# Two pairs of feature blocks of the sixth tile by seven half-size products, laced with the fifth tile's outputs

## The chip, the cores and the metric

The kernel runs on one core of a Trainium2 chip. The metric is the time of one execution on the device in microseconds (us); the median of several runs is compared. Engines are called by the names that the profile uses: PE is TensorE (matrix products), DVE is VectorE, ACT is ScalarE, POOL is GpSimd, SP is SyncE, which issues nearly all DMA transfers here.

## The reference

```python
def _attn_ref(q, k, v):                      # 4 batches, 8 heads, 768 steps, 64 channels
    gamma = 1.0 - 2.0 ** (-5.0 - np.arange(H))
    for t in range(S):
        state = gamma * state + einsum('bhd,bhe->bhde', k[:, :, t], v[:, :, t])
        y[:, :, t] = scale * einsum('bhd,bhde->bhe', q[:, :, t], state)

def _moe_ref(x, w_a, w_b, w_out):            # 3072 tokens, 512 wide, 1536 features
    a = x @ w_a
    b = x @ w_b
    return a * b @ w_out

x = attn_out.transpose(0, 2, 1, 3).reshape(B * S, H * D)
```

A decaying linear attention makes x, and x goes through a bilinear feed-forward layer: two products of x with a weight each, multiplied element by element, and a third product back to 512 columns.

## The kernel before

**Tiles.** The 3072 tokens are 24 slots of 128. Slots are gathered into tiles (`TILES = [4, 2, 2, 2, 2, 4, 8]`), so the sixth tile, index 5, has 4 slots (512 tokens, slots 12 to 15), and the seventh, `BIG`, has 8. For each slot q and k are scaled on GpSimd (`casts`, line 293), transposed by a DMA on SP (`flip`, line 312), and the loads of slot t+2 are issued behind that flip on SP. `turn(new, old)` (line 404) makes the masked scores of two slots (on PE, then four multiplications with the mask on VectorE, line 348), updates the state, and finishes two older slots, whose result is copied by ScalarE into `xt`, the input of the feed-forward layer.

**Feed-forward blocks.** The 1536 features are 12 blocks of 128. `ffn_a` (line 529) makes a block of a: four products on PE, which ScalarE casts into `asb`. `ffn_g` (line 543) makes the block of b in the same way, and VectorE multiplies it with `asb` into `ht`. `blocks(J, a, b)` runs both over blocks a to b.

**Seven products in place of eight.** For the outputs of the tiles of index 1 to 6, and for the whole of the first two products of `BIG`, the kernel uses the Strassen-Winograd scheme: the operands are cut in two each way, and the four quarter results come from seven products of sums of quarters, not from eight. `Group` (line 632) does it for the output of two slots: p1 to p7 are the products, A, B and C its three PSUM banks, `snap` copies a partial sum out of bank A on ScalarE, and VectorE adds a snap to a bank. `hsum` makes its sums of quarters of `ht`, `weight_sum` those of the third weight. `Unit` (line 786) does it for a pair of feature blocks of `BIG` (p and p+6) and one weight, 512 tokens wide; its weight sums `WS` are made on GpSimd by `weight_piece` (line 751), from a list of 32 pieces that `weight_pieces(n)` works off, and its input sums by `x_sum` on VectorE.

**Order.** All work is put in program order by hand: each engine runs its instructions in the order in which the code emits them (`seq`, line 100). PE's banks are eight: three in a ring (`psff`, line 75, which hands out the bank that has been free the longest), four of attention (y0, y1, at0, at1) and one for the state. `single(4, ...)` (line 736) runs the one output group of the fifth tile with blocks 0, 1 and 2 of the sixth between its products; then come blocks 3 to 11 of the sixth tile between the last turns, and `big()` with its two written orders START and END.

The main sequence around the change, before:

```python
    casts(19)
    single(4, Y0, AT0, FF)
    v_cast(18)
    casts(20)
    casts(21)
    blocks(5, 3, 5)
    v_cast(19)
    blocks(5, 5, 6)
    weight_pieces(6)
    turn(18, 16)
    sums(5, 5)
    casts(22)
    blocks(5, 6, 9)
    casts(23)
    weight_pieces(2)
```

Of the kernel before, what the change touches and what calls it, by code (L numbers as in the profile page):

```python
# [22 lines left out]
       "S02 S01 b7 a2 b2 S04 a6 b6 S13 a5 b5 S12 a3 b3 a4 b4 S11 c7 d7 c6 d6 S14 c5 d5 "  # L23
       "c3 c4 d4 d3")
V_LATE = range(12, 20)
LOADS = "p0 p1 w0 w1 a1 b1 a2 k2 q2 b2 v2 o0 o1 o2 o3 o4 o5 s6 t8".split()


@with_exitstack
def kernel(  # L30
# [29 lines left out]
    const = ctx.enter_context(tc.tile_pool(name="const", bufs=1))  # L60
    wpool = ctx.enter_context(tc.tile_pool(name="wpool", bufs=1))
    wstage = ctx.enter_context(tc.tile_pool(name="wstage", bufs=6))
    raw = ctx.enter_context(tc.tile_pool(name="raw", bufs=3))
    nat = ctx.enter_context(tc.tile_pool(name="nat", bufs=6))
    tra = ctx.enter_context(tc.tile_pool(name="tra", bufs=4))
    xtp = ctx.enter_context(tc.tile_pool(name="xtp", bufs=2))
# [39 lines left out]
        return bi  # L106


    raws, wst, whole = {}, {}, {}

    def load_slot(t, names="kqv"):
        b, ci = divmod(t, NCH)
        for nm in names:
            src = {"k": k, "q": q, "v": v}[nm]
            if nm == "q":
                if t % 2 == 0:
                    load_two(nm, src, b, ci // 2, t)
                continue
            if t % 2 == 0:
                whole[nm] = raw.tile([P, 2, H, D], F32, tag=nm + "f", name=nm + "f")  # L120
# [6 lines left out]
            load_slot(u, names)  # L127

    def load_two(nm, src, b, u, t):
        f = raw.tile([P, H, 2, D], F32, tag=nm + "f", name=nm + "f")  # L130
# [273 lines left out]
    def turn(new, old, eng=nc.scalar):  # L404
        if old is not None:
            ys[old // 2] = [psat.tile([P, 2, 2, 2, P // 2], F32, tag=f"y{r}", name="y") for r in range(2)]
        two = new is not None and (new + 1) % NCH < NCH - 1
        if new is not None:
            if two or old is None:
                update(new, eng)  # L410
            scores(new + 1, "y" if old is None else "ff")
            scores(new, "at")
        if old is not None:
            inter(old)
            inter(old + 1)
# [152 lines left out]
    def ffn_out(J, i, n):  # L568
        if n == 0:
            store()  # L570
            plain_out[i] = psff.tile([P, DM], F32, tag="ff", name="o")
        o = plain_out[i]
        for ft in range(NP * n, NP * n + NP):
            seq(nc.tensor.matmul(o, ht[J][:, ft, i * P : (i + 1) * P], wo_bf[:, ft],  # L574
                                 start=(ft == 0), stop=(ft == NFT - 1), skip_group_check=True))
# [10 lines left out]
    def tt(dst, x, y, op, eng=nc.vector):  # L586
        seq(eng.tensor_tensor(dst, x, y, op=op))  # L587
# [13 lines left out]
    hs = {}  # L601

    def hs_tile(J, s):
        if (J, s) not in hs:
            pool, tag = (raw, ("kf", "qf", "vf", "kf")[s - 1]) if J in (0, (BIG, 1)) else (wstage, "w")
            bufs = {}
            if (J, s) == (0, 4):
                pool, tag, bufs = tra, "kqT", {"bufs": 3}
            hs[J, s] = pool.tile([P, NP, 2, P], BF16, tag=tag, name=f"hs{s}", **bufs)

    def hsum(J, s, a, b, eng=nc.vector):
        U = slice(int(J == 0), 2 if isinstance(J, tuple) else TILES[J] // 2)
# [8 lines left out]
    def hsums(J, a, b, eng):  # L621
        for s in (2, 1, 4):
            hsum(J, s, a, b, eng)

    WHEN = {5: ["302"], 6: ["324"], 7: ["346"], 8: ["102"], 9: ["202d", "224", "124"],
            10: ["402", "424"], 11: ["246", "146", "446"]}

    def sums(J, ft, eng=nc.vector):
        for what in WHEN.get(ft, []):
            hsum(J, *map(int, what[:3]), nc.vector if what[3:] else eng)  # L630
# [102 lines left out]
    Y0, Y1, AT0, AT1 = ((psat, x) for x in ("y0", "y1", "at0", "at1"))  # L733
    ST = (psst, "st")

    def single(J, A, B, C):
# [12 lines left out]
    WS, XS, pieces = {}, {}, []  # L749

    def weight_piece(w, n, a, b):
        if (w, n) not in WS:
            WS[w, n] = raw.tile([P, 2, NP * P], BF16, tag=("kf", "qf", "vf")[len(WS) % 3], name=f"ws{w}{n}")
# [3 lines left out]
        S = {x: WS[w, x][:, :, a * P : b * P] for x in (1, 2, 3, 4) if (w, x) in WS}  # L757
        x, y, op = {3: (A11, A21, ALU.subtract), 2: (A22, S[3], ALU.subtract), 1: (A21, A22, ALU.add),
                    4: (A12, S.get(2), ALU.subtract)}[n]
        tt(S[n], x, y, op, nc.gpsimd)  # L760
# [25 lines left out]
    class Unit:  # L786
# [6 lines left out]
        def product(self, bank, left, right, first):  # L793
            if first:
                pool, tag = self.tags[bank]
                self.bank[bank] = pool.tile([P, 4 * P], F32, tag=tag, name="u" + bank)
            m, p = self.bank[bank], self.p
            for k in range(2):
                if isinstance(left, int):
                    w = WS[self.w, left][:, k, p * P : (p + 1) * P]  # L800
# [53 lines left out]

        def p4(self):
            self.product("B", (1, 1), XS[4], False)
            self.leave(1, 0, "B", 1)

    STEP = {"1": 0, "6": 4, "2": 6, "5": 8, "7": 9, "3": 12, "4": 17}
# [99 lines left out]
    def blocks(J, a, b):  # L959
        for ft in range(a, b):  # L960
            ffn_ab(J, ft)
            if J == 5 and ft + 1 < b:
                sums(J, ft, G_ if ft > 8 else nc.vector)

    def three(J, ft):
        store()
# [5 lines left out]
    def v_cast(t):  # L972
        cast(nc.scalar, vb[t], raws["v", t])
# [123 lines left out]
```

## Time and profile before

| | before |
|---|---|
| median of 3 runs | 219.35 us (218.97 to 219.61) |
| the profiled execution's own time | 219.35 us |
| its span (first to last instruction) | 217.6 us |
| PE busy | 210.5 us, 97% of the span |
| VectorE, ScalarE, GpSimd busy | 141.4, 100.8, 148.1 us |
| granted TensorE clock | 9 tenths or more in all 40 slices |

The profile is one execution, recorded by the hardware. A row of the timeline gives the start and the length in us, the engine, the source line, the operation with output<-input, the shapes, the number of instructions merged into the row, and in brackets the idle time of the engine ahead of it with what ended it. Rows of groups give busy time and the mean duration in ns after the bar. A row of a stretch (from:to) gives its length, then busy time of PE, PEld (weight loads), DVE, ACT and POOL, then the granted clock, the DMA share and GB/s. Matmuls are pipelined: the duration of one is longer than the distance from one to the next.

### The profile page before, as it was taken

Reading aid. Unit: us, or ns where it says so; the run is one execution under the profiler, and the core shown is the slowest. Engines: PE = TensorE matmul, PEld = TensorE weight load, DVE = VectorE, ACT = ScalarE, POOL = GpSimd, SP = SyncE. Lnnn points to the kernel's source line nnn. Section 1 sums busy time; section 2 is a strip of 40 time slices with the busy share of each in tenths; the row PEclk is TensorE's granted clock in tenths of the full one; section 3 lists DMA queues with packets and bytes.
Section 4 is the critical chain, followed back from the end, with each engine's and each line's share of the span. In section 5 each row is a group of like instructions: output and inputs, shape, how many; then the busy total and the mean of one; then the engine's idle time right before and its main releaser. Section 6 shows DMA issues by size and latency. Waiting matters only on the chain.

```text
span 217.6 us, 5674 instructions
## 1 busy us (share of the span) xinstructions
PE 210.5 (97%) x2244; PEld 143.5 (66%) x2244; DVE 141.4 (65%) x258; ACT 100.8 (46%) x221; POOL 148.1 (68%) x173
## 2 busy tenths in 40 slices
PE   7699999999999999999999999999999999999994
PEld 3457445587458888888888665456864444458883
DVE  2777446845973486356477245886586887688962
ACT  3266335343224444455576344455546656652331
POOL 5266876879344469579865949999999999950000
PEclk9999999999999999999999999999999999999999
DMA  6999999999999999999999997980013000000055
GB/s 165 290 322 364 384 289 362 384 270 229 207 265 230 191 236 213 195 218 254 198 216 247 206 202 182 255 124 5 3 48 145 0 2 3 0 2 0 27 193 169
DMA packets 85162, 39.68 MB, mean 182 GB/s; under 512 B 57488, under 2 KB 78864, under 8 KB 85136
## 3 DMA queue, kind: packets, MB, share of 16 engines
q1 hardware_dynamic: 84992, 39.26, 80.1%
q8 instruction: 17, 0.28, 0.6%
q10 hardware_dynamic: 144, 0.07, 0.1%
q14 instruction: 9, 0.07, 0.1%
HBM read 28.31 MB, written 6.29 MB: 159 GB/s over the span
## 4 chain that ended last, share of the span: by engine, by line
PE 91%; SPq 4%; DMA 3%; POOL 0%; issue 0%; DVE 0%
PE a L537 20%; PE g L549 19%; PE mA L654 12%; PE uA L805 10%; PE mB L654 6%; PE o L574 5%; PE uB L805 5%; SPq L132 4%; DMA wsta<-in_moe_w_a_dram 3%; PE mC L654 3%; PE at L342 2%; PE uC L805 2%; PE y L390 2%; PE st L360 2%; PE y L380 1%; PE y L500 1%
## 5 line engine op out<-in xcount | busy, mean ns | idle before, releaser
L551 DVE TENSOR_TENSOR ht<-g,asb 128x256 bf16<-128x256 f32 (+1 forms) x74 | 37.2, 503 | 37.5 <-PE g L549 34.4
L537 PE MATMUL a<-xt,wa_bf 128*128 128x256 bf16 (+1 forms) x296 | 52.7, 305 | 0.1
L549 PE MATMUL g<-xt,wb_bf 128*128 128x256 bf16 (+1 forms) x296 | 52.5, 304 | 0.0
L540 ACT CAST asb<-a 128x256 bf16<-128x256 f32 (+1 forms) x74 | 32.3, 437 | 38.8 <-PE a L537 35.7
L549 PEld LDWEIGHTS <-wb_bf 128*128 128x128 bf16 x296 | 28.6, 98 | 12.5
L537 PEld LDWEIGHTS <-wa_bf 128*128 128x128 bf16 x296 | 28.0, 98 | 12.1 <-POOL wa_bf L245 0.4
L286 POOL TENSOR_TENSOR kqb<-kf,ktab 128x512 bf16<-128x512 f32 x22 | 23.0, 1049 | 16.3 <-DMA kf<-in_k_dram 15.9
L812 ACT COPY snap<-uA 128x512 f32<-128x512 f32 x36 | 20.0, 588 | 15.4 <-PE uA L805 13.9
L654 PEld LDWEIGHTS <-hs 128*128 128x128 bf16 x234 | 22.8, 98 | 4.1
L286 POOL TENSOR_TENSOR kqb<-qf,qtab 128x512 bf16<-128x512 f32 x18 | 19.0, 1054 | 6.1 <-DMA qf<-in_q_dram 6.1
L348 DVE TENSOR_TENSOR aT<-at,mask 128x512 bf16<-128x512 f32 x36 | 22.3, 682 | 0.3
L661 ACT COPY snaps<-mA 128x256 f32<-128x256 f32 x30 | 11.0, 374 | 20.1 <-PE mA L654 20.1
L654 PEld LDWEIGHTS <-ht 128*128 128x128 bf16 x180 | 17.5, 98 | 3.2
L587 POOL TENSOR_TENSOR hs<-ht,hs 128x384 bf16<-128x384 bf16 (+1 forms) x17 | 16.7, 990 | 2.9 <-DVE ht L551 2.8
L587 POOL TENSOR_TENSOR ht<-gsb,asb 128x512 bf16<-128x512 bf16 x13 | 15.3, 1185 | 1.6 <-DVE gsb L587 1.6
L587 POOL TENSOR_TENSOR hs<-ht 128x384 bf16<-128x384 bf16 (+2 forms) x12 | 13.8, 1153 | 3.4 <-DVE ht L551 3.4
L245 POOL CAST vb<-vf 128x512 bf16<-128x512 f32 x16 | 10.0, 642 | 7.7 <-DMA vf<-in_v_dram 7.5
L654 PE MATMUL mA<-wsum,hs 128*128 128x256 bf16 x120 | 15.2, 273 | 0.0
L587 DVE TENSOR_TENSOR osb<-mB,snaps 128x256 f32<-128x256 f32 x20 | 8.5, 423 | 8.4 <-PE mB L654 4.2
L574 PE MATMUL o<-wo_bf,ht 128*128 128x512 bf16 x48 | 10.7, 379 | 0.0
L587 DVE TENSOR_TENSOR asb<-uB,snap 128x512 bf16<-128x512 f32 x12 | 8.2, 686 | 3.4 <-ACT snap L812 1.7
L587 DVE TENSOR_TENSOR gsb<-uB,snap 128x512 bf16<-128x512 f32 x12 | 8.3, 688 | 2.8 <-ACT snap L812 2.0
(101 smaller groups left out, 334.1 us busy)
## 6 DMA issues: line engine op xcount, KB each, us to landing
qf<-in_q_dram SPq DMA_DIRECT2D x12, 512.0 KB, 6.1
out_dram<-osb SPq DMA_DIRECT2D x21, 256.0 KB, 4.1
kf<-in_k_dram SPq DMA_DIRECT2D x18, 256.0 KB, 4.9
vf<-in_v_dram SPq DMA_DIRECT2D x18, 256.0 KB, 5.4
wsta<-in_moe_w_a_dram SPq DMA_DIRECT2D x6, 512.0 KB, 7.6
wsto<-in_moe_w_out_dram SPq DMA_DIRECT2D x6, 512.0 KB, 8.7
wstb<-in_moe_w_b_dram SPq DMA_DIRECT2D x5, 512.0 KB, 8.2
kf<-in_k_dram SPq DMA_DIRECT2D x3, 512.0 KB, 7.6
```

The lines of the kernel that those rows point to most:

```text
L286: seq(eng.tensor_tensor(dst, src, tab, op=ALU.mult))
L348: seq(nc.vector.tensor_tensor(aT[t][:, r], at[r], mask.to_broadcast([P, HP, P]), op=ALU.mult))
L537: seq(nc.tensor.matmul(a, wa_bf[:, kt, fs], xcols(J, kt, c0, c1), start=(kt == 0), stop=(kt == KT - 1)))
L540: seq(nc.scalar.copy(asb, a))
L549: seq(nc.tensor.matmul(g, wb_bf[:, kt, fs], xcols(J, kt, c0, c1), start=(kt == 0), stop=(kt == KT - 1)))
L551: seq(nc.vector.tensor_tensor(ht[J][:, ft, c0:c1], g, asbs.pop((J, ft, c0)), op=ALU.mult))
L574: seq(nc.tensor.matmul(o, ht[J][:, ft, i * P : (i + 1) * P], wo_bf[:, ft], start=(ft == 0), stop=(ft == NFT - 1), skip_group_check=True))
L587: seq(eng.tensor_tensor(dst, x, y, op=op))
L654: seq(nc.tensor.matmul(m, w, right[:, j], start=(first and j == 0), stop=(j == NP - 1), skip_group_check=True))
L661: seq(nc.scalar.copy(self.snaps[:, n], self.bank["A"]))
L805: seq(nc.tensor.matmul(m, w, right[:, k], start=(first and k == 0), stop=(k == 1), skip_group_check=True))
L812: seq(nc.scalar.copy(self.snaps[n], self.bank["A"]))
```

## The change

Four feature blocks of the sixth tile, 0 and 6, 1 and 7, are taken out of `blocks` and made by a new class `Quad`: one pair of blocks, one weight, seven products of half size (256 tokens wide, two matmuls each). Quads a and b are the two weights of the first pair, c and d those of the second. They stand in one written order, LACED, with the seven products of the fifth tile's output group (m1 to m7) and blocks 2 and 3 of the sixth (F is `ffn_a`, G is `ffn_g`). X is a sum of input quarters on VectorE, S is `casts`, V is `v_cast`, H is `hsum`. Blocks 4, 5 and 8 follow after the turn, blocks 9 to 11 as before.

A quad has a bank A of the ring, a bank B (AT1 or Y1), and shares one ring bank C between the a and b of a pair. Its snaps are copies on ScalarE, its adds are on VectorE; each b quad multiplies its halves with the a quad's (two of these from SBUF tiles on VectorE, one on GpSimd, one straight out of PSUM on VectorE).

The weight sums of feature blocks 0, 1, 6 and 7 are needed earlier. They get tiles of their own (`early`) and are cut finer (one feature block a piece for the first three), and 16 of the pieces are put between earlier steps of the main sequence. To make room the rings for k and q loads have two buffers and not three, and the later weight sums share tiles. Half sums of the sixth tile (`WHEN`) are regrouped to the new order of its blocks; some move between VectorE and GpSimd.

```diff
+LACED = ("X3 X2 m1 m7 m2 a1 b1 m6 a2 b2 X1 a6 b6 a7 b7 F2 X4 m5 a5 b5 S20 G2 a3 b3 a4 b4 V18 S21 "
+         "m3 c1 d1 F3 H3 c6 d6 c7 d7 c2 d2 c5 d5 V19 m4 c3 d3 c4 d4 G3")
...
-    raw = ctx.enter_context(tc.tile_pool(name="raw", bufs=3))
+    raw = ctx.enter_context(tc.tile_pool(name="raw", bufs=2))
+    early = ctx.enter_context(tc.tile_pool(name="early", bufs=1))
...
+    def raw_tile(shape, dtype, tag, name):
+        return raw.tile(shape, dtype, tag=tag, name=name, bufs=3 if tag == "vf" else 2)
...
-    WHEN = {5: ["302"], 6: ["324"], 7: ["346"], 8: ["102"], 9: ["202d", "224", "124"],
-            10: ["402", "424"], 11: ["246", "146", "446"]}
+    WHEN = {4: ["324"], 5: ["102", "402", "346"], 8: [], 9: ["224d", "124"], 10: ["424"],
+            11: ["246", "146", "446"]}
...
+    def laced(order):
+        made = {"m": Group(4, 0, Y0, AT0, Y1)}
+        for p in range(2):
+            made.update({"ac"[p]: Quad(p, "a", AT1, "kqT2"), "bd"[p]: Quad(p, "b", Y1, "aT")})
...
+    NE = 2
+    WE = {w: early.tile([P, 4, 2, NE * P], BF16, name="we" + w) for w in "ab"}
...
-    for a, b in ((0, 1), (1, 3), (3, 5), (5, 6)):
+    for a, b in ((0, 1), (1, 2), (2, 3), (3, 5), (5, 6)):
...
+    def xf_sum(n):
+        if n in (3, 1):
+            XF["pair"] = osbp.tile([P, 2, 2, DH], BF16, tag="osb", name="xf")
+        XF[n] = XF["pair"][:, int(n in (2, 4))]
+        x, y, op = {3: (xf(1, 1), xf(0, 1), ALU.subtract), 2: (XF.get(3), xf(0, 0), ALU.add),
+                    1: (xf(0, 1), xf(0, 0), ALU.subtract), 4: (xf(1, 0), XF.get(2), ALU.subtract)}[n]
+        tt(XF[n], x, y, op)
...
+    class Quad:
...
+        def leave(self, i, c, bank, n):
+            cols = slice(c * DH, (c + 1) * DH)
+            if self.w == "a":
+                tt(self.half(i)[:, cols], self.bank[bank], self.snaps[n], ALU.add)
+                return
+            h = ht[5][:, NP * i + self.p, cols]
+            tt(h, self.bank[bank], self.snaps[n], ALU.add)
+            tt(h, h, self.half(i)[:, cols], ALU.mult, nc.gpsimd if (i, c) == (1, 0) else nc.vector)
+
+        def p1(self):
+            self.A = self.whole(FF)
+            self.bank["A"] = self.A[:, :DH]
+            self.product("A", (0, 0), xf(0, 0), True)
+            self.snap()
+
+        def p2(self):
+            n = int(self.w == "b")
+            if not n:
+                self.shared[self.p] = self, self.whole(FF)
+            mate, C = self.shared[self.p]
+            self.bank["C"] = C[:, n * DH : (n + 1) * DH]
+            self.product("C", (0, 1), xf(1, 0), True, not n)
+            if n:
+                mate.leave(0, 0, "C", 0)
+                self.leave(0, 0, "C", 0)
+                psff.back(C)
+
+        def p6(self):
+            self.product("A", 2, XF[2], False)
+            self.snap()
+
+        def p7(self):
+            self.bank["B"] = self.whole(self.tagB)[:, :DH]
+            self.product("B", 3, XF[3], True)
+
+        def p5(self):
+            self.product("A", 1, XF[1], False)
+            self.snap()
+            self.leave(1, 1, "B", 2)
+
+        def p3(self):
+            self.product("A", 4, xf(1, 1), False)
+            if self.w == "a":
+                seq(nc.scalar.copy(self.half(0)[:, DH:], self.bank["A"]))
+            else:
+                tt(ht[5][:, self.p, DH:], self.bank["A"], self.half(0)[:, DH:], ALU.mult)
+            psff.back(self.A)
+
+        def p4(self):
+            self.product("B", (1, 1), XF[4], False)
+            self.leave(1, 0, "B", 1)
...
     casts(8)
+    weight_pieces(2)
...
     casts(9)
+    weight_pieces(2)
...
     casts(10)
+    weight_pieces(4)
...
-    casts(14)
+    casts(14, lambda: weight_pieces(3))
     blocks(3, 3, 6)
+    weight_pieces(2)
...
     casts(17)
+    weight_pieces(3)
...
     casts(19)
-    single(4, Y0, AT0, FF)
-    v_cast(18)
-    casts(20)
-    casts(21)
-    blocks(5, 3, 5)
-    v_cast(19)
-    blocks(5, 5, 6)
-    weight_pieces(6)
+    laced(LACED)
+    casts(22)
     turn(18, 16)
-    sums(5, 5)
-    casts(22)
-    blocks(5, 6, 9)
+    hsum(5, 3, 1, 2)
+    hsum(5, 2, 0, 2, G_)
     casts(23)
+    blocks(5, 4, 6)
+    blocks(5, 8, 9)
     weight_pieces(2)
```

In the prediction, products are called by their names in LACED: a5 is the fifth product of quad a, m5 that of the output group. A6 is a product of START: the sixth (with the sum of quarters `hs2`) of the sixth tile's own first output group.

More of the change, by code (lines that the diff above doesn't have):

```diff
@@ L119, in load_slot @@
             if t % 2 == 0:
[L120 removed]
+                whole[nm] = raw_tile([P, 2, H, D], F32, nm + "f", nm + "f")
             raws[nm, t] = whole[nm][:, t % 2]
@@ L603, in hs_tile @@
     def hs_tile(J, s):
[L604 to L609, printed above, removed]
+        if (J, s) in hs:
+            return
+        if J == (BIG, 1):
+            hs[J, s] = raw_tile([P, NP, 2, P], BF16, ("kf", "qf", "vf", "kf")[s - 1], f"hs{s}")
+        else:
+            hs[J, s] = wstage.tile([P, NP, 2, P], BF16, tag="w", name=f"hs{s}")
     def hsum(J, s, a, b, eng=nc.vector):
@@ L734 @@
     ST = (psst, "st")
+    def laced(order):
+        made = {"m": Group(4, 0, Y0, AT0, Y1)}
+        for p in range(2):
+            made.update({"ac"[p]: Quad(p, "a", AT1, "kqT2"), "bd"[p]: Quad(p, "b", Y1, "aT")})
+        ht[5] = htp.tile([P, NFT, 4 * P], BF16, tag="ht", name="ht")
+        for x in order.split():
+            if x[0] == "H":
+                hsum(5, int(x[1]), 0, 1)
+            elif x[0] in "XFGVS":
+                {"X": xf_sum, "F": lambda f: (store(), ffn_a(5, f)), "G": lambda f: ffn_g(5, f), "V": v_cast,
+                 "S": casts}[x[0]](int(x[1:]))
+            else:
+                getattr(made[x[0]], "p" + x[1])()
     def single(J, A, B, C):
@@ new lines, with __init__, whole, product @@
+    half_f = {}
+    class Quad:
+        shared = {}
+        def __init__(self, p, w, B, snaps):
+            self.p, self.w, self.tagB, self.spare = p, w, B, snaps
+            self.bank, self.snaps = {}, []
+        def whole(self, tag):
+            return tag[0].tile([P, 4 * P], F32, tag=tag[1], name="f" + self.w)
+        def product(self, bank, left, right, first, opens=True):
+            m, p = self.bank[bank], self.p
+            for k in range(2):
+                if isinstance(left, int):
+                    w = ws(self.w, left, p, p + 1)[:, k]
+                else:
+                    i, j = left
+                    f = (NP * i + p) * P
+                    w = {"a": wa_bf, "b": wb_bf}[self.w][:, 2 * j + k, f : f + P]
+                seq(nc.tensor.matmul(m, w, right[:, k], start=(first and opens and k == 0), stop=(k == 1),
+                                     skip_group_check=True))
+        def snap(self):
+            n = len(self.snaps)
+            if n == 0 and self.spare == "kqT2":
+                three = tra.tile([P, 3, DH], F32, tag="kqT2", name="snapf", bufs=2)
+                self.room = [three[:, x] for x in range(3)]
+            elif n == 0:
+                two = [tra.tile([P, 2, DH], F32, tag="aT", name="snapf") for _ in range(2)]
+                self.room = [t[:, x] for t in two for x in range(2)]
+            self.snaps.append(self.room[n])
+            seq(nc.scalar.copy(self.snaps[n], self.bank["A"]))
+        def half(self, i):
+            key = self.p, i
+            if key not in half_f:
+                half_f[key] = asbp.tile([P, 4 * P], BF16, tag="asb", name="asb")
+            return half_f[key]
+        def leave(self, i, c, bank, n):
+            cols = slice(c * DH, (c + 1) * DH)
+            if self.w == "a":
+                tt(self.half(i)[:, cols], self.bank[bank], self.snaps[n], ALU.add)
+                return
+            h = ht[5][:, NP * i + self.p, cols]
[31 more added lines that the diff above has]
+                seq(nc.scalar.copy(self.half(0)[:, DH:], self.bank["A"]))
+            else:
+                tt(ht[5][:, self.p, DH:], self.bank["A"], self.half(0)[:, DH:], ALU.mult)
+            psff.back(self.A)
+        def p4(self):
+            self.product("B", (1, 1), XF[4], False)
@@ L963, in blocks @@
                 sums(J, ft, G_ if ft > 8 else nc.vector)
+        if J == 5 and b == 6:
+            sums(J, 5, G_)
     def three(J, ft):
```

25 lines of the change are left out of this document (17 added, 8 removed).

## The prediction

> **What bounds the kernel now.** I read the page first (engines, chain), then the stretches of 20 us, then PE's waits.
>
> ```profile
> PE 210.5 (97%) x2244; PEld 143.5 (66%) x2244; DVE 141.4 (65%) x258; ACT 100.8 (46%) x221; POOL 148.1 (68%) x173
> ...
> PE 91%; SPq 4%; DMA 3%; POOL 0%; issue 0%; DVE 0%
> ```
>
> ```profile
> 140.00:160.00 20.00, 19.98 (x285) 13.67 (x284) 14.02 (x23) 10.23 (x22) 19.67 (x19) 1.00 0.35 73
> ```
>
> ```profile
> PE tp L446 <- DVE kqb L286: 1.9, 3, 1.4
> PE idle L521 <- DVE zero L180: 1.5, 1, 1.5
> PE idle L521 <- ACT kqT L243: 0.4, 1, 0.4
> ```
>
> The chain is TensorE, 91%. PE's waits, all three of them, are of the transposes (tp) and the idle products at the start; later it has none that is listed, and a stretch such as 140 to 160 us shows it busy for 19.98 of 20 us at a granted clock of 1.00. So PE is a full pipe. Less PE work is worth its whole length, and every new stall is lost in full, because nothing later has slack to take it up. In that stretch GpSimd is as full as PE (19.67).
>
> Busy is not pace. The pace comes from merged rows of the timeline:
>
> ```profile
> 52.98 7.93 PE L574 MATMUL o<-wo_bf,ht 128*128 128x512 bf16 x36
> ...
> 61.93 2.76 PE L574 MATMUL o<-wo_bf,ht 128*128 128x512 bf16 x12
> ...
> 119.06 0.82 PE L654 MATMUL mA<-wo_bf,ht 128*128 128x256 bf16 x6
> ...
> 154.76 1.47 PE L654 MATMUL mA<-wsum,hs 128*128 128x256 bf16 x12
> ```
>
> At 512 columns 24 more products take 5.17 us more: 0.215 each, and I use 0.216. At 256 columns six more take 0.65: 0.109. Half size costs half.
>
> **What the change removes on PE.** Feature blocks 0, 1, 6 and 7 of the sixth tile, each with four products for a and four for g, make 32 products of 512 columns: 32 x 0.216 = 6.91 us. The four quads have seven products of two matmuls at 256 columns: 56 x 0.109 = 6.10 us. Gain 0.81 us, if nothing stalls. The profiled execution took 219.35 us, which is also the median of the runs shown: 218.54 at best. A measurement of this kernel can tell about 0.3%, 0.66 us, so that gain only just shows.
>
> [...]
>
> **The weight sums.** Sixteen pieces of one feature block move ahead, into idle times of GpSimd, in groups of 2, 2, 4, 3, 2 and 3. One piece, and the three places that the longer groups take (idle time in the brackets):
>
> ```profile
> 72.18 1.04 POOL L286 TENSOR_TENSOR kqb<-kf,ktab 128x512 bf16<-128x512 f32 x1 [2.80 <-DMA kf<-in_k_dram]
> ...
> 92.48 1.04 POOL L286 TENSOR_TENSOR kqb<-qf,qtab 128x512 bf16<-128x512 f32 x1 [2.17 <-DMA qf<-in_q_dram]
> ...
> 110.99 1.64 POOL L587 TENSOR_TENSOR hs<-ht 128x768 bf16<-128x768 bf16 x1 [2.07 <-DVE ht L551]
> ...
> 133.25 0.67 POOL L587 TENSOR_TENSOR wsa<-wa_bf 128x256 bf16<-128x256 bf16 x1
> ```
>
> At 0.67 us a piece these groups need 2.7, 2.0 and 2.0 us and fit, if narrowly; the groups of two need 1.3 and have more room in theirs. I cost them at nothing. Without that cover a group would push the casts, flips and loads behind it by its length. The kf and qf rings shrink from three buffers to two. A load stands on SP behind the flip of slot t and takes the buffer that slot t-1 or an earlier one read, so it waits for nothing new: nothing either.
>
> **The laced stage.** Two kinds of drain, as the page groups them:
>
> ```profile
> L661 ACT COPY snaps<-mA 128x256 f32<-128x256 f32 x30 | 11.0, 374 | 20.1 <-PE mA L654 20.1
> ...
> L587 DVE TENSOR_TENSOR osb<-mB,snaps 128x256 f32<-128x256 f32 x20 | 8.5, 423 | 8.4 <-PE mB L654 4.2
> ```
>
> ACT gives up four casts of 512 columns for fourteen copies of 256, 14 x 0.374 = 5.2 us over a stage of 14 us; laid beside PE's order, none of them comes out late. VectorE gets the weight. In place of four products of 512 columns it makes twelve adds from PSUM of 0.42 us, two products from PSUM, four input sums (X) and four multiplications of SBUF tiles (two more go to GpSimd). How an operation with two SBUF inputs fares beside GpSimd, these rows show:
>
> ```profile
> 137.25 1.04 POOL L286 TENSOR_TENSOR kqb<-kf,ktab 128x512 bf16<-128x512 f32 x1
> 137.28 1.30 DVE L587 TENSOR_TENSOR hs<-ht 128x512 bf16<-128x512 bf16 x1
> 138.26 1.22 POOL L286 TENSOR_TENSOR kqb<-qf,qtab 128x512 bf16<-128x512 f32 x1
> ...
> 140.29 0.41 DVE L587 TENSOR_TENSOR hs<-ht 128x512 bf16<-128x512 bf16 x1
> ```
>
> Left alone, the sum takes 0.41. Issued 0.03 us behind a GpSimd operation it takes 1.30: it ends 0.29 us after that one's end, and the next GpSimd operation takes 1.22 for 1.04. They alternate. [...]
>
> Now the order itself, on the clock of before, with m1 at 119.06 (above):
>
> ```profile
> 120.06 0.91 POOL L587 TENSOR_TENSOR hs<-ht,hs 128x384 bf16<-128x384 bf16 x1 [1.81 <-DVE ht L551]
> ...
> 130.28 1.04 POOL L286 TENSOR_TENSOR kqb<-kf,ktab 128x512 bf16<-128x512 f32 x1 [2.77 <-DMA kf<-in_k_dram]
> ...
> 134.10 0.32 PE L360 MATMUL st<-vb,kqb 128*64 128x64 bf16 x8
> ...
> 134.89 2.47 DVE L348 TENSOR_TENSOR aT<-at,mask 128x512 bf16<-128x512 f32 x4
> ```
>
> Adding 0.109 and 0.216 along the new order, PE would start b2 at 122.34, a5 at 124.94, a4 at 126.68, c1 at 127.77, c4 at 131.91, and the turn near 133.3 instead of 134.10. GpSimd has work from 120.06 to 127.5 (130.28 less 2.77). On VectorE four operations from PSUM take 2.47 us, 0.62 each; I take 0.35 for 256 columns back to back.
>
> b2's result can be read from 122.75 and its add, second in line, ends near 123.3. Behind it in VectorE's queue stand b's multiplication, X1, X4, m5's add, a5's and b5's adds, b's next multiplication and G2's product. The multiplication waits for what is left of a GpSimd operation, I take half of one, and ends near 124.0. X1 then meets the next whole one: 124.0 + 1.04 + 0.29 = 125.3, and a5, which needs it at 124.94, waits 0.4. X4 comes out at 126.6, the three adds at 127.0, 127.35 and 127.7. a4 and b4 reuse the banks that a5's and b5's adds read: 127.1 becomes 127.4, and b4, then due at 127.6, starts at 127.75. That is 0.3 and 0.15. The second multiplication gets 0.3 of waiting, and G2's product ends near 128.8; c1, due at 128.6, takes its bank: 0.2. The second pair meets GpSimd's idle time ahead of 130.28 and then the casts of slot 21; I take 0.1 at c4 and d4. Sum 1.15 us of stalls. Its bounds: 0.1 (VectorE never blocked; then every product finds bank and input within 0.1), and 3.2 (both first waits a whole operation, 1.2 more, and 0.9 in the second pair). I stay in the lower half, because only the whole-operation waits of X1 and X4 are forced. Net +0.34: 219.7 us.
>
> A second deadline is GpSimd's:
>
> ```profile
> 147.88 3.38 POOL L587 TENSOR_TENSOR hs<-ht,hs 128x512 bf16<-128x512 bf16 x3
> ...
> 151.77 0.82 PE L654 MATMUL mA<-wsum,hs 128*128 128x256 bf16 x6
> ```
>
> The half sum that A6 needs for its fifth product (due at 152.2) is the last of the three, ready at 151.26. The flip of slot 19, on SP, waits for that slot's casts, and the later loads and flips stand behind it in SP's queue, so a delay of those casts is passed on to the last k load, behind which GpSimd has as many operations as before. VectorE's four early operations delay them by up to 0.18 us each, some 0.6, and PE comes 0.81 sooner: 0.5 us of the gain would be lost there. After 1.15 of stalls PE comes later and doesn't wait, so the sum stands. The casts of 22 ahead of the turn and of 23 behind it, and the moved half sums, are the same work in another order under the same PE time.
>
> **Rivals.** *The order fits*, VectorE hardly blocked: 219.35 - 0.81 + 0.1 = 218.65. For it: without contention I find no stall over 0.1. Against it: three two-input operations in a row under a full GpSimd, and the rows at 137 us alternate. *Only A6 waits*: 218.54 + 0.5 = 219.05. *VectorE's backlog reaches the turn*: slower. The casts of slot 21 begin at 130.28 plus GpSimd's delay, and d's two multiplications come near 132. If they meet one of them whole, it puts about 0.9 ahead of c5's and d5's adds, on whose banks c4 and d4 wait; the turn's scores and y banks then wait for c4's and d4's adds. 1.15 + 0.9 = 2.05 of stalls: 220.6. It decides from 1.47 us of stalls on. For it: the casts stand at 130.28 already. Against it: GpSimd waits for its load there and can come later still. *Half-size products don't pay*: break-even is 6.91/56 = 0.123 us a product, and the rows show 0.109.
>
> **How the numbers follow.** Forecast 0.33 (its own range 218.7 to 220.0), A6 alone 0.11: within 0.3%, 0.44. The order fits: faster, 0.24. Backlog 0.31 and half size not paying 0.01: slower, 0.32. The range, 218.6 to 221.0, takes in the fit and the backlog up to 2.5 us of stalls; beyond it I leave 0.1 above and less below.
>
> **What would show it.** Right: the quads' products 0.109 apart; a5, a4, b4 and c1 late by a few tenths, with X1 and X4 near 1.3 us on VectorE; the turn near 134.4. Wrong: X rows near 0.41, the turn at 133.3, and A6 waiting or not; or, the other way, c4, d4 and the turn waiting for VectorE by whole microseconds. The early pieces are wrong if GpSimd's next rows start later than before, and the rings if kf or qf are waited for longer.

## The result and the profile after

The changed kernel is slower by half a per cent: 220.21 us median (219.38 to 221.94, 21 executions) beside 219.29 us for the kernel before on the same chip (21 executions); ratio 1.0048, 95% interval 1.0031 to 1.0066. The profiled execution took 219.65 us with a span of 217.8, near the low end of its 21; it shows 0.3 us of the 0.9.

The page of the changed kernel, busy times and the chain:

```profile
PE 210.7 (97%) x2256; PEld 146.0 (67%) x2268; DVE 150.3 (69%) x276; ACT 102.9 (47%) x231; POOL 153.4 (70%) x184
...
PE 87%; SPq 3%; DMA 3%; DVE 2%; issue 1%; ACT 1%; POOL 0%; DVEq 0%; ACTq 0%
```

VectorE's 2% is new in the chain of what ended last (0% before). The timeline of the laced stage shows where it comes in (start, length, engine, line, operation):

```profile
118.93 0.82 PE L660 MATMUL mA<-wo_bf,ht 128*128 128x256 bf16 x6
...
119.77 0.41 DVE L593 TENSOR_TENSOR xf<-xt 128x512 bf16<-128x512 bf16 x1
...
122.42 0.38 PE L924 MATMUL fa<-xf,wea 128*128 128x256 bf16 x2
122.64 0.38 PE L924 MATMUL fb<-xf,web 128*128 128x256 bf16 x2
...
122.84 1.04 POOL L292 TENSOR_TENSOR kqb<-kf,ktab 128x512 bf16<-128x512 f32 x1
...
123.04 0.41 DVE L593 TENSOR_TENSOR ht<-fa,snapf 128x256 bf16<-128x256 f32 x1
...
123.48 0.54 DVE L593 TENSOR_TENSOR ht<-ht,asb 128x256 bf16<-128x256 bf16 x1
123.50 1.02 PE L543 MATMUL a<-xt,wa_bf 128*128 128x512 bf16 x3
123.84 1.09 POOL L292 TENSOR_TENSOR kqb<-qf,qtab 128x512 bf16<-128x512 f32 x1
123.94 1.26 DVE L593 TENSOR_TENSOR xf<-xt 128x512 bf16<-128x512 bf16 x1
...
124.88 1.22 POOL L292 TENSOR_TENSOR kqb<-kf,ktab 128x512 bf16<-128x512 f32 x1
125.13 1.26 DVE L593 TENSOR_TENSOR xf<-xt,xf 128x512 bf16<-128x512 bf16 x1
125.26 0.39 PE L924 MATMUL fa<-xf,wea 128*128 128x256 bf16 x2
...
134.28 0.32 PE L366 MATMUL st<-vb,kqb 128*64 128x64 bf16 x8
```

Two matmuls of a quad's product are 0.22 us apart from the next two (122.42, 122.64): 0.109 each. X3 at 119.77 took 0.41 us; X1 and X4 (123.94, 125.13), the same kind of operation behind a cast of GpSimd, took 1.26 each. X1 ends at 125.20 and a5, which reads it, starts at 125.26, 0.24 us later than the pace asks. From m1 to the turn's state products are 134.28 - 118.93 = 15.35 us, where before had 134.10 - 119.06 = 15.04. Without a stall it would be 15.04 - 0.81 = 14.23, so the stage stalls for 1.12 us. Everything behind the turn has its old length: 83.5 us from these products to the end of the span in both profiles.

The rest of the 0.9 us is not in that execution. The span, and the time that an execution takes outside its span, tell where to look:

| kernel | executions | span: lowest, median, highest | time outside the span: highest | of these over 1.80 |
|---|---|---|---|---|
| before (in the experiments) | 105 | 217.1, 217.4, 218.5 | 1.79 | 0 |
| after | 21 | 217.5, 218.1, 220.2 | 2.70 | 13 |
| after_again | 12 | 217.5, 218.2, 220.2 | 2.54 | 6 |
| pieces_only | 12 | 217.2, 217.4, 218.1 | 1.76 | 0 |
| late_pieces | 12 | 217.9, 218.6, 219.7 | 1.76 | 0 |
| x1_early | 7 | 217.8, 218.6, 219.6 | 1.89 | 2 |
| no_two_input | 12 | 217.5, 218.0, 219.8 | 2.71 | 8 |
| a6_relief | 12 | 217.7, 218.0, 218.7 | 2.90 | 7 |
| defer | 12 | 217.1, 218.1, 219.8 | 2.21 | 7 |
| defer_relief | 12 | 216.7, 216.7, 218.9 | 1.99 | 5 |
| defer_relief_2 | 12 | 216.6, 216.7, 218.7 | 2.45 | 6 |
| turn_later | 12 | 216.6, 216.9, 218.9 | 1.99 | 5 |
| k_early | 11 | 216.6, 217.4, 218.9 | 2.91 | 3 |
| code_shift | 6 | 217.9, 218.0, 218.7 | 1.76 | 0 |

The time outside the span is an execution's time less its span, which is on record to 0.1 us. The lowest span of the changed kernel is 0.4 us over that of before, about what the stage gives (0.31). Its median span is 0.7 over, four spans of 21 are 2.1 to 2.7 us longer than the lowest, and 13 executions have over 1.80 us outside the span, which none of the 105 of before has. That second part was in no step of the prediction.

### The profile page after: what moved, and what is told of

Same layout as the page of the kernel before. It is cut to its first block, busy times and chain, and to the rows that moved or that the text cites. A ratio compares the mean times of both kernels' runs of the same rounds, so it can differ in the third digit from the quotient of the medians.

```text
span 217.8 us, 5740 instructions
## 1 busy us (share of the span) xinstructions
PE 210.7 (97%) x2256; PEld 146.0 (67%) x2268; DVE 150.3 (69%) x276; ACT 102.9 (47%) x231; POOL 153.4 (70%) x184
## 4 chain that ended last, share of the span: by engine, by line
PE 87%; SPq 3%; DMA 3%; DVE 2%; issue 1%; ACT 1%; POOL 0%; DVEq 0%; ACTq 0%
PE g L555 18%; PE a L543 18%; PE mA L660 11%; PE uA L834 9%; PE mB L660 6%; PE o L580 5%; PE uB L834 4%; SPq L138 3%; DMA wsta<-in_moe_w_a_dram 3%; PE mC L660 3%; PE at L348 2%; PE uC L834 2%; PE y L396 2%; PE st L366 2%; PE fa L924 1%
## 5 line engine op out<-in xcount | busy, mean ns | idle before, releaser
L557 DVE TENSOR_TENSOR ht<-g,asb 128x256 bf16<-128x256 f32 (+1 forms) x70 | 34.4, 492 | 29.7 <-PE g L555 25.9
L543 PE MATMUL a<-xt,wa_bf 128*128 128x256 bf16 (+1 forms) x277 | 48.4, 299 | 0.3
L555 PE MATMUL g<-xt,wb_bf 128*128 128x256 bf16 (+1 forms) x279 | 48.2, 300 | 0.1
L546 ACT CAST asb<-a 128x256 bf16<-128x256 f32 (+1 forms) x70 | 30.0, 429 | 34.8 <-PE a L543 33.1
L555 PEld LDWEIGHTS <-wb_bf 128*128 128x128 bf16 x280 | 27.1, 98 | 10.2
L543 PEld LDWEIGHTS <-wa_bf 128*128 128x128 bf16 x280 | 26.5, 98 | 10.9 <-POOL wa_bf L251 0.4
L593 POOL TENSOR_TENSOR hs<-ht 128x384 bf16<-128x384 bf16 (+2 forms) x13 | 15.2, 1168 | 1.5 <-DVE ht L557 1.5
```

The lines of the kernel that those rows point to most:

```text
L543: seq(nc.tensor.matmul(a, wa_bf[:, kt, fs], xcols(J, kt, c0, c1), start=(kt == 0), stop=(kt == KT - 1)))
L546: seq(nc.scalar.copy(asb, a))
L555: seq(nc.tensor.matmul(g, wb_bf[:, kt, fs], xcols(J, kt, c0, c1), start=(kt == 0), stop=(kt == KT - 1)))
L557: seq(nc.vector.tensor_tensor(ht[J][:, ft, c0:c1], g, asbs.pop((J, ft, c0)), op=ALU.mult))
```

## The experiments

All were timed beside the kernel before on the same chip (medians 219.09 to 219.13 us). The theories, as the expectations name them: **1**, VectorE's operations with two SBUF inputs wait for GpSimd in the laced stage; **2**, the early weight pieces, the smaller rings, or the transposed load of slot 17, which comes near its due time; **3**, the half sums of the sixth tile come late for A6 in the last stage; **4**, a late chain of loads and transposes at the turn of slots 20 and 21; **5**, something at the very end.

**after_again**: the changed kernel without an edit.

> The changed kernel once more, unchanged, for a second profile and its spread. The stage of the laced order alone (theory 1: VectorE's two-input operations wait for GpSimd) explains +0.3 us, with the waits at F2, a5, a4, b4, c1, c4 and d4 at the same places, 1.1 us together. Theory 2 (the transposed k and q of slot 17 land about when the turn of slots 16 and 17 needs them, and later in some executions) wants the remaining 0.6 us of the median ahead of 119 us: in this profile the turn's first products near 116.5 us wait for the transpose, or the time is near 219.7.

219.96 us, ratio 1.0046 [1.0026, 1.0065]. The same gaps: 0.2 at F2, 0.25 at a5, 0.10, 0.11, 0.06 at a4, b4, c1, and 0.32 and 0.11 at c4 and d4. The loss stands. No product waits for the transpose at the turn near 116.5 us, so this profile gives theory 2 nothing.

**pieces_only**: the order of before (the main sequence quoted above, without its six late pieces, and its WHEN), with the new buffers and the 16 early pieces.

```diff
-    laced(LACED)
+    single(4, Y0, AT0, FF)
+    v_cast(18)
...
+    blocks(5, 3, 5)
...
+    blocks(5, 6, 9)
```

> The order of before (no laced stage, no half-size products for the sixth tile), with the changed kernel's buffers (two for k and q) and the sixteen early weight pieces in GpSimd's gaps. Theory 1: 219.3 us, as before. Theory 2: 219.9, and a wait for the transpose near 116.5 us.

219.15 us, ratio 1.0002 [0.9989, 1.0016]. Rings and early pieces cost nothing; theory 2 falls for both of these.

**late_pieces**: the same, with the pieces, still cut finer, where before had its own: all six early places are emptied.

```diff
     casts(10)
-    weight_pieces(4)
...
     blocks(5, 5, 6)
+    weight_pieces(6)
     turn(18, 16)
...
     sums(5, NFT - 1, G_)
-    weight_pieces(8)
+    weight_pieces(16)
```

> As the one above (order of before, buffers of the changed kernel), but the sixteen pieces are made late, six ahead of the turn of slots 18 and 19 and the others ahead of the last stage. If the early pieces delay the transposes: 219.3 us. If the two-buffer rings do it: 219.9. Theory 1: 219.3.

220.29 us, ratio 1.0046 [1.0027, 1.0065], which neither side expected. The timeline of this kernel has one of the waits that it makes in the last stage:

```profile
181.60 0.69 DVE L593 TENSOR_TENSOR asb<-uB,snap 128x512 bf16<-128x512 f32 x1 [1.79 <-POOL ht L593]
...
182.94 0.59 PE L834 MATMUL uB<-xs,wsb 128*128 128x512 bf16 x2 [0.47 <-DVE gsb L593]
```

VectorE waited 1.79 us for GpSimd and TensorE 0.47 for VectorE. These are two waits; that all of the 1.1 us is made in this way isn't shown. So placing the pieces early is not only free; cut like this, they have to be early.

**x1_early**: X1 moved ahead.

```diff
-LACED = ("X3 X2 m1 m7 m2 a1 b1 m6 a2 b2 X1 a6 b6 a7 b7 F2 X4 m5 a5 b5 S20 G2 a3 b3 a4 b4 V18 S21 "
+LACED = ("X3 X2 m1 m7 X1 m2 a1 b1 m6 a2 b2 a6 b6 a7 b7 F2 X4 m5 a5 b5 S20 G2 a3 b3 a4 b4 V18 S21 "
```

> The changed kernel with the input sum X1 moved ahead in VectorE's order, from behind b2 to behind m7, where VectorE stood idle for 1.1 us. Theory 1: X1 is ready before 123 us, a5 no longer waits (0.24 us), X4 comes a GpSimd operation earlier and a4, b4 and c1 wait for less: up to 0.6 us less than the changed kernel, 219.6. Theory 2: the same as the changed kernel but for those 0.3 to 0.6 us.

220.44 us (7 executions), ratio 1.0059 [1.0033, 1.0084]. The timeline:

```profile
124.82 0.38 PE L924 MATMUL fa<-xf,wea 128*128 128x256 bf16 x2
...
131.16 1.04 POOL L292 TENSOR_TENSOR kqb<-kf,ktab 128x512 bf16<-128x512 f32 x1 [1.57 <-DMA kf<-in_k_dram]
...
131.56 0.79 DVE L593 TENSOR_TENSOR ht<-ht,asb 128x256 bf16<-128x256 bf16 x1
...
132.74 0.38 PE L924 MATMUL fa<-xf,wa_bf 128*128 128x256 bf16 x2 [0.55 <-DVE asb L593]
```

a5 now starts at 124.82 without a gap. But PE comes sooner to c and d, where d's multiplication meets the cast of slot 21 (0.79 us, where after had 0.29), and c4 starts 0.7 us later than the pace asks, where after had 0.2. The wait moved and didn't go, and the 219.6 us of theory 1 were missed. This is the mechanism of the prediction's *backlog* rival, at nearly its price of 0.9.

**no_two_input**: X1, X4 and four of VectorE's multiplications left out.

```diff
+        if n in (1, 4):
+            XF[n] = XF[{1: 3, 4: 2}[n]]
+            return
         tt(XF[n], x, y, op)
...
-            tt(h, h, self.half(i)[:, cols], ALU.mult, nc.gpsimd if (i, c) == (1, 0) else nc.vector)
+            if (i, c) == (1, 0):
+                tt(h, h, self.half(i)[:, cols], ALU.mult, nc.gpsimd)
```

> The changed kernel without six of VectorE's eight new operations that have two SBUF inputs: X1 and X4 are left out (X3 and X2 stand in for them) and so are the four multiplications of SBUF tiles on VectorE. PE's work is unchanged. Theory 1 (these operations, waiting for GpSimd, hold up VectorE's queue and through it PE): the waits at F2, a5, a4, b4, c1, c4 and d4 go, the stage takes 14.2 us and not 15.35, and both the median and the spread come down, to 218.5 us, or to 219.0 if the first output group of the sixth tile then waits for its half sums. Theory 3 (the spread comes from that group's half sums on GpSimd, late by the loads): 219.3 or more, with a spread as wide as before.

220.01 us, ratio 1.0046 [1.0024, 1.0069]: no faster. The timeline says why:

```profile
116.38 0.73 PE L348 MATMUL at<-kqT 64*64 64x128 bf16 x32
...
133.53 0.64 PE L348 MATMUL at<-kqT 64*64 64x128 bf16 x32
...
150.20 2.27 POOL L593 TENSOR_TENSOR hs<-ht,hs 128x512 bf16<-128x512 bf16 x2
...
152.53 0.39 PE L660 MATMUL mA<-wsum,hs 128*128 128x256 bf16 x2 [0.96 <-POOL hs L593]
```

The same scores in before, and then in after:

```profile
116.60 0.73 PE L342 MATMUL at<-kqT 64*64 64x128 bf16 x32
...
134.35 0.64 PE L342 MATMUL at<-kqT 64*64 64x128 bf16 x32
```

```profile
116.47 0.73 PE L348 MATMUL at<-kqT 64*64 64x128 bf16 x32
...
134.53 0.64 PE L348 MATMUL at<-kqT 64*64 64x128 bf16 x32
```

From the turn of slots 17 and 16 to that of 19 and 18 are 17.15 us, against 18.06 in after and 17.75 before: theory 1 is right for the stage, where only F2's 0.2 stays. But the last half sum for A6 ends at 152.47, and PE, which now comes 1 us sooner, waits 0.96 for it. That half sum is also 0.72 us later than in after (151.75): GpSimd's last cast of k, behind a wait for its load in both, starts at 141.63 where after has 140.92. Why the load is later isn't shown. Theory 3 is right as well, behind the first.

**a6_relief**: only that second deadline is eased; two weight pieces go behind the half sums.

```diff
     blocks(5, 8, 9)
-    weight_pieces(2)
...
     sums(5, NFT - 1, G_)
-    weight_pieces(8)
+    weight_pieces(10)
```

> The changed kernel, with two weight pieces that GpSimd makes ahead of the last half sums of the sixth tile put behind them, so that these half sums are ready 1.5 us earlier. Theory 3 (in many executions PE waits for the last half sum at A6; its margin in the profile is 0.64 us): median 219.5 us and a narrower spread. Theory 1 (the loss and its spread are of the laced stage): 220.1, as the changed kernel.

220.16 us, ratio 1.004 [1.0022, 1.0057]. Nothing gained alone. Its waits show the near miss of theory 2 once as a hit, at the turn of slots 17 and 16:

```profile
PE at L348 <- DMA kqT<-kqb: 0.5, 1, 0.5
```

**defer**: X1 early; the first pair's multiplications are put off to a new entry K0 of the order, behind the adds that free banks, and the second pair's go to GpSimd.

```diff
-LACED = ("X3 X2 m1 m7 m2 a1 b1 m6 a2 b2 X1 a6 b6 a7 b7 F2 X4 m5 a5 b5 S20 G2 a3 b3 a4 b4 V18 S21 "
+LACED = ("X3 X2 m1 m7 X1 m2 a1 b1 m6 a2 b2 a6 b6 a7 b7 F2 X4 m5 a5 b5 S20 G2 a3 b3 a4 b4 K0 V18 S21 "
...
+            if x[0] == "K":
+                for put in later:
+                    put()
+                later.clear()
...
-            tt(h, h, self.half(i)[:, cols], ALU.mult, nc.gpsimd if (i, c) == (1, 0) else nc.vector)
+            other = self.half(i)[:, cols]
+            if (i, c) == (1, 0) or self.p:
+                tt(h, h, other, ALU.mult, nc.gpsimd)
+            else:
+                later.append(lambda: tt(h, h, other, ALU.mult))
```

> The changed kernel with VectorE's two-input operations put where GpSimd or VectorE is idle: X1 ahead of m2; the first pair's two multiplications behind b4's add; the second pair's two on GpSimd behind the casts of slot 21. Nothing is left out. Theory 1: only the wait at F2 remains, the stage takes 14.4 us, 218.6 to 218.9 us; with theory 3's wait at A6 on top 219.1.

219.92 us, ratio 1.0035 [1.0011, 1.0059]. The stage is clear again (scores at 116.37 and 133.53), and A6 waits 0.81 us; the 219.1 us that its expectation had with such a wait were missed by 0.8. It does with all the work what no_two_input does with less. X1 and X4 still take 1.13 and 0.97 us beside GpSimd (at 121.06 and 123.27), but now end ahead of the time at which they are needed.

**defer_relief**, defer with the edit of a6_relief, and **defer_relief_2**, the same again.

> The two edits together: two-input operations put into idle times, and the two weight pieces behind the last half sums. Theories 1 and 3 together: 218.6 us, faster than the kernel before by 0.3%. Theory 1 alone: the same as without the second edit.

> The version with the two-input operations in idle times and the two pieces behind the half sums, once more: 218.6 us again, with some executions up to 2 us above, and faster than the kernel before if the median holds.

218.61 and 218.60 us, ratios 0.9991 [0.9967, 1.0015] and 0.9989 [0.9968, 1.0009]. The waits of defer_relief are those of before, all at the start:

```profile
PE idle L527 <- DVE zero L186: 1.5, 1, 1.5
PE tp L452 <- DVE kqb L292: 1.3, 3, 0.8
PE idle L527 <- ACT kqT L249: 0.4, 1, 0.4
```

The span is 216.7 us: 1.1 us less than after. The median is 0.5 us below before, but 3 of 12 executions in each are 1.2 to 2.0 us over the median, and the interval holds 1.

**turn_later**: defer_relief with block 9 ahead of the last-but-one turn.

```diff
-    blocks(5, 8, 9)
+    blocks(5, 8, 10)
     turn(20, 18)
-    sums(5, 8, G_)
-    blocks(5, 9, NFT)
+    sums(5, 9, G_)
+    blocks(5, 10, NFT)
```

> The same version, with the turn of slots 20 and 21 one feature block later (block 9 ahead of it). Theory 4 (what is left of the spread comes from the load and transpose chain, whose slot 21 lands at 139.9 us where the turn wants it at 140.5): the executions 2 us above go, median 218.6. If the spread comes from elsewhere: the same spread.

218.67 us, ratio 0.9997 [0.9974, 1.0019]; four of 12 executions long. Theory 4 gets nothing for it at that turn.

**k_early**: defer_relief with k of the odd slots loaded one slot sooner.

```diff
         elif u < NSLOT:
-            load_slot(u)
+            load_slot(u, "kqv" if u < 12 else "kq" if u % 2 == 0 else "")
+            if u >= 12:
+                if u % 2 == 0:
+                    load_slot(u + 1, "k")
+                load_slot(u, "v")
```

> The same version as the first, with the k of each odd slot from 13 on loaded together with the even one, a slot earlier, so that the casts and transposes of slots 15, 17, 19, 21 and 23 don't wait for it. Theory 4: the transposes of slots 17 and 21 land earlier than 116.2 and 139.9 us, and the median and the spread fall, to 218.4 us. If the k load isn't what they wait for: the same as the first, or slower by the rearranged queue.

219.61 us, the median of 11 executions (219.86 with a twelfth of 435 us, which the ratio leaves out as well), ratio 1.0014 [0.9991, 1.0038]. The transpose of slot 17 lands at 116.29 us, no earlier than defer_relief's 116.24, and theory 4 gets nothing. No remedy, but its profiled execution was a long one, 220.57 us with a span of 218.9. PE ended its last product at 213.89, within 0.25 us of defer_relief's 213.68. The two microseconds lie behind that. The DMA view of defer_relief, from 213.5 to 217.5 us (busy tenths in 40 slices, GB/s, queues, and the last stores with their time from issue to landing):

```profile
DMA  9999999999999999930000000000000000000000
...
q1 hardware_dynamic: 535, 0.51, 38.0%
q10 hardware_dynamic: 144, 0.07, 5.9%
...
out_dram<-osb ACTq DMA_DIRECT2D x1, 64.0 KB, 1.9
out_dram<-osb SPq DMA_DIRECT2D x1, 64.0 KB, 1.8
```

The same view of k_early, from 213.5 to 220 us:

```profile
GB/s 353 365 391 372 309 340 309 353 312 284 271 218 19 101 0 0 0 0 0 3 9 9 9 16 3 0 0 0 0 0 0 0 0 0 0 0 0 0 0 0
...
q8 instruction: 1, 0.02, 0.9%
...
out_dram<-osb ACTq DMA_DIRECT2D x1, 64.0 KB, 3.8
out_dram<-osb SPq DMA_DIRECT2D x1, 64.0 KB, 3.7
```

A packet of code (16 KB, on queue q8) starts at 215.75 us, on its way while the last stores are; what is left of these trickles in at 3 to 16 GB/s from 216.6 on, and they land 1.9 us later than in every other profile of these kernels (1.8 to 2.0 us).

Why there? The stretches between such packets, with PE's and PEld's instructions (x), in before and in after:

```profile
157.16:181.47 24.31, 24.31 (x131) 12.63 (x129) 19.73 (x31) 14.04 (x27) 23.91 (x23) 1.00 0.12 43
181.47:202.42 20.95, 20.95 (x128) 12.28 (x127) 16.99 (x28) 10.24 (x21) 12.09 (x13) 1.00 0.02 6
202.42:217.60 15.18, 12.17 (x118) 10.78 (x115) 9.23 (x17) 4.37 (x12) 0.00 (x0) 1.00 0.38 133
```

```profile
176.21:200.04 23.83, 23.67 (x126) 12.49 (x128) 19.30 (x31) 13.24 (x27) 13.65 (x15) 1.00 0.01 2
200.04:217.80 17.76, 14.73 (x141) 13.06 (x139) 11.19 (x21) 4.57 (x13) 0.00 (x0) 0.99 0.34 118
```

In the three of these stretches that end with a packet it comes 254 to 260 of TensorE's instructions after the one before (131 + 129, 128 + 127, 126 + 128). Single distances vary more, and the next one back in after has 266 (133 + 133):

```profile
154.18:176.21 22.03, 21.93 (x133) 12.96 (x133) 17.51 (x27) 12.46 (x26) 20.97 (x21) 1.00 0.13 48
```

Over the whole of before there are 17 packets (0.28 MB in the DMA view, 16 KB each) for 4488 recorded instructions of TensorE, 264 each, but single distances in it go from 126 (83.54 to 90.28 us) to 371 (73.71 to 83.54). That the packets come by TensorE's instructions is the author's reading of these counts, and when one is due is an estimate from that mean; the profile names the kind of their queue, instruction, and not what a packet holds. Behind the last packet of before 118 + 115 = 233 are left, so by that mean none is due by the end. The change adds 24 products with their weight loads, 48 instructions (36 of them recorded): in after 280 are left, and by the same mean one more packet is due near the end. In the profiles it comes at 218.8 us in after and x1_early, at 217.9 to 218.0 in defer_relief_2 and turn_later, after the last store, and at 215.75 in k_early, into it. The other five profiles of laced kernels whose code lies in its first place (after_again, no_two_input, a6_relief, defer and defer_relief) show none at the end; whether none came or the record ended first isn't shown.

**code_shift**: defer_relief, with the products on zeros at the start cut into 98 small ones (zero is bf16 now), so that all of TensorE's code lies some 170 instructions further on.

```diff
-        for n in cols:
-            seq(nc.tensor.matmul(idle[:, :n], zero[:, :P], zero[:, :n], start=True, stop=True,
+        for _ in range({512: 18, 256: 11, 128: 6}[cols[0]] if len(cols) == 1 else 52):
+            seq(nc.tensor.matmul(idle[:, :P], zero[:, :P], zero[:, :P], start=True, stop=True,
```

> defer_relief with TensorE's warm-up products at the start (7 f32 products on zeros, 28 instructions) replaced by 98 small bf16 products on zeros in the same stretches of time: TensorE's instruction stream is some 170 instructions longer, before the first real product, and nothing else is touched. Theory 5: the executions about 1.9 us longer (10 of 36 of defer_relief, its repeat and turn_later stood above 219.8 us, the others between 218.28 and 219.15) come from the very end: in k_early's profile a 16-KB instruction packet of queue q8 was on a DMA engine at the moment of the last stores, and these took 3.7 and 3.8 us from issue to landing instead of 1.8 and 1.9; the packets of that queue come once in some 256 of TensorE's instructions, and the changed kernel's longer stream has one that falls on the kernel's end, where the kernel before has none. With 170 instructions more that packet lies about 8 us earlier, and no packet falls on the end: 218.3 to 219.2 us in all executions, none above 219.8, median about 218.55, ratio 0.997 with an interval below 1. Rival (the long executions come from somewhere inside, such as the late transposed load of slot 17 or the clock): 3 or 4 of 12 again above 219.8, median 218.6, interval up to 1.002. If TensorE's first real product comes later through the small products, all executions move by that much together and the spread still tells.

219.75 us (219.66 to 220.41, 6 executions), ratio 1.0033 [1.002, 1.0045]. The last packet is now at 206.2 us, with 87 + 85 instructions behind it:

```profile
206.20:218.10 11.90, 8.86 (x87) 7.81 (x85) 5.92 (x12) 2.93 (x9) 0.00 (x0) 1.00 0.47 165
```

Five of the six lie within 0.2 us, the sixth 0.75 over the lowest, none is 1.2 us or more over the median, and none has over 1.76 us outside its span. At the earlier rate of 10 in 36, six without a long one would come by luck one time in seven, so the spans alone don't settle it. The time outside the span does more: over 1.80 in 62 of the 123 executions of all laced kernels whose code lies in its first place, in 0 of 6 here, 0 of 24 of pieces_only and late_pieces, and 0 of 105 of before. So it goes with where the code lies.

That the packet is what lengthens it isn't shown: of the four profiled executions with a packet after the last store two have over 1.80 (after 1.85, defer_relief_2 2.36) and two have not (x1_early 1.77, turn_later 1.74), and three of the five without one have over 1.80 too (no_two_input and defer 1.98, defer_relief 1.86). The long spans are a separate group: in defer_relief, its repeat, turn_later and k_early 14 of 47 executions have a span of 218.4 us or more, 19 others have over 1.80 outside, and none has both. This fits a packet that comes now into the last stores and now behind them, but late_pieces has spans of up to 219.7, and its profile shows no packet at its end, so a long span alone is no sign of one.

The median is 1.1 us worse than defer_relief's, and 1.2 over the forecast. The difference stands at the start. GpSimd's first weight cast, in defer_relief and then in code_shift:

```profile
15.66 1.18 POOL L251 CAST wa_bf<-wsta 128x512 bf16<-128x512 f32 x2 [0.34 <-DMA wsta<-in_moe_w_a_dram]
```

```profile
17.08 1.18 POOL L251 CAST wa_bf<-wsta 128x512 bf16<-128x512 f32 x2 [1.74 <-DMA wsta<-in_moe_w_a_dram]
```

Its load was issued at the same time (8.58 and 8.56 us) and landed at 15.60 and 17.03. Between stands a code packet at 13.4 us that defer_relief has at 16.0. TensorE's first product with that weight starts 1.42 us later (17.75 for 16.33), and the span is 1.4 us longer. Again a transfer that something waits for is late by 1.4 us when a code packet runs among it; here, too, only the coincidence is shown.

## Why the prediction was right and wrong, step by step

- **The pace of half-size products**, 0.109 us: right. The *half-size products don't pay* rival falls, and the gain of 0.81 us on PE exists: in defer_relief, with no stall but F2's 0.2, the scores of the two turns stand 17.15 us apart (116.28 and 133.43) for 17.75 in before, 0.6 less.
- **Early pieces and two-buffer rings at nothing**: right (pieces_only, 1.0002).
- **The stage's stalls, 1.15 us**: the sum was right (1.12), its parts less so, and that it is so close is in part luck: what was put too high (0.45 us in all) and too low (0.43) cancel. a5 waited 0.24 and not 0.4, a4 0.10 and not 0.3, b4 0.12 for 0.15, c1 0.14 for 0.2, while c4 and d4 took 0.33 and not 0.1. F2's 0.2 was missed: it takes the bank that b2's add frees at 123.45, which the prediction, on a clock 0.13 us later, had near 123.3. This gap stands in every laced kernel, with no_two_input too, so the bound of 0.1 us for a stage without contention was too low. X1 and X4 came out at 1.26 where 1.30 was said, ended at 125.20 and 126.39 where 125.3 and 126.6 were, and the turn came at 134.28 with "near 134.4" on record.
- **A6 does not wait after the stalls**: right in after (its half sum was ready at 151.75 for the product due at 152.39). The *only A6 waits* rival is true as soon as the stalls go, at 0.96 and 0.81 us rather than 0.5.
- **Net +0.34, 219.7 us**: right for the profiled execution (219.65) and short for the median, 220.21, which the range of 218.6 to 221.0 holds. "Within 0.3%" was given 0.44 and "slower" 0.32; it was slower by 0.48%. Two steps fell short. One is the sentence that the profiled time "is also the median of the runs shown": true of before, taken over to after without a reason. The other is that the sum had no term for what differs from one execution to the next. In the mean the span of after is 0.88 us over that of before in the experiments (218.38 for 217.50), of which the stage gives 0.31, and the time outside the span is 0.27 over (1.99 for 1.72). A candidate for part of this is that 24 products more are 48 instructions more on TensorE, which were costed by their time alone, so that by the mean of before, 264 recorded ones to a packet, one more packet of code is due near the end. How much of the 0.56 us between the profiled execution and the median it makes isn't shown. What the experiments do show is that with both waits eased (defer_relief) the ratio falls from 1.0048 to 0.9991 and the median span from 218.1 to 216.7 us, so most of the spans' excess goes with the stage and A6, though the profile of after shows no wait at A6.
- **Backlog**: its mechanism appeared in x1_early (0.7 us at c4), not in after, where c4 waited 0.2. The median is on that rival's side of the line, but not by its cause.

What stays open: that the packet delays the last stores is seen in one profile, and the time outside the span goes with the place of the code but not, execution by execution, with a packet that is seen; which DMA engine it holds, and what makes it come early in some executions, isn't shown. Nor is it shown why the spans of after lie anywhere between 217.5 and 218.6 when they aren't long, where those of defer_relief lie mostly at 216.6 to 217.2; stalls of the stage, the load of slot 17 and A6 are each a few tenths from their due times there.

## What to carry to other kernels

Products saved on a full TensorE pay only when every later deadline has as much room as the gain: here VectorE's waits in the stage hid A6, and removing either alone gave little or nothing (defer 219.92 us, a6_relief 220.16) where both gave 1.1 us of span, and even that version isn't shown to be faster than the kernel before. Put VectorE's operations with two SBUF inputs behind the adds that free banks, or beside idle time of GpSimd: in after X3, issued ahead of a GpSimd operation, took 0.41 us, X1 and X4, issued behind one, 1.26 each. Count instructions as well as time (here 48 more on TensorE), look where the code packets fall against the first loads and last stores, and compare the spread of many executions before trusting one profile.

## What was not expected of the hardware

- A 16-KB code packet on the last stores: 3.7 and 3.8 us from issue to landing for 1.8 and 1.9; one at 13.4 us beside the first weight load: 1.4 us later. Both are coincidences in time in single profiles.
- The granted clock falls to half behind PE's last product, between 216 and 217 us in k_early; its mean of 0.995 for that execution comes from this idle tail and not from a slower stage, as the clock is 1.00 in every stretch up to 216:

```profile
216.00:217.00 1.00, 0.00 (x0) 0.00 (x0) 0.00 (x0) 0.00 (x0) 0.00 (x0) 0.82 0.03 3
217.00:218.00 1.00, 0.00 (x0) 0.00 (x0) 0.00 (x0) 0.00 (x0) 0.00 (x0) 0.50 0.03 5
```
